# Seven block products for the first expert's second output product, with sums made by accumulating transfers

## The chip, the cores and the metric

The kernel runs on one core of one Trainium2 chip. The metric is device time in microseconds of one launch. The engines are TensorE (matmul), VectorE, ScalarE, GpSimd and SyncE; the last issues the loads. In the profile they are PE (and PEld for its weight loads), DVE, ACT, POOL and SP.

## The reference

Attention with a causal mask (2 batches, 12 heads, 448 positions, 64 per head) gives x, 896 tokens by 768. Two experts follow, one on the other's output:

```python
h = x @ w_in                    # 768 -> 2048
g = h - np.tanh(h)
x = g @ w_out                   # 2048 -> 768, the first expert
a, b = x @ w_a, x @ w_b         # 768 -> 1536 each
out = (a * b) @ w_out2          # 1536 -> 768, the second expert
```

q, k and v are float32. The experts' weights are 64-bit floats; the kernel loads their upper bytes and puts float32 values together from their bits.

## The kernel before

Every float32 operand is split into a high half (float32r) and a low half, and a product of two operands is three matmuls: high by high, high by low, low by high. ScalarE makes the high half (L292 for weights, L649 for activations), VectorE the low half (L301, L650).

The first expert's 2048 hidden columns are taken in three groups of 4, 6 and 6 chunks of 128 (`GROUPS1`, L69). For each group the hidden product is made, then its part of the output product, which is added up in `part` in SBUF. The loop over the groups is at L799. This text is about the output product of the second group, 6 chunks.

The hidden products of the second and third group use seven block products in place of eight: two row blocks (384 of the 768 inputs), two column blocks (two chunks) and two token blocks (the batches B0 and B1, 448 tokens each). A unit is a pair of chunks; `turn` (L775) makes one of its seven products, 9 matmuls of 448 columns. Which product adds to which PSUM bank is in it. `combine` (L239) makes the sums of weight blocks on VectorE, `x_sums` those of x. `gate` (L747) makes tanh on ScalarE, the difference on VectorE and then both halves of g.

The output product of the second group is plain: for each of 6 output blocks `dm` and for two pieces of tokens (512 and 384), 6 chunks by 3 matmuls, and then an addition of the PSUM bank to `part` on VectorE (`add`, L745). Its weights are whole blocks, split at a stroke (128x768).

Weights go through a chain. `load_part` (L185) loads a tile in two halves on SyncE's queue. `magnitude` (L194) makes an fp16 part on ScalarE and `bits` (L214) joins it with the lower bits on VectorE, into one of 4 buffers `t`. `split_high` and `split_low` then write the halves into one of 5 pairs of buffers `wh`, `wl`, each pair with place for two split blocks of 384 or one whole of 768. `plan` is the order in which blocks are split. `advance`, called once per product, makes one step of each. A `t` buffer is reused when `last_use` of its tile has been split.

PSUM has 8 banks with four names: `s` 4, `t` 2, `o` 1, `h` 1. `next_bank` gives them out in a fixed turn. Eight buffers `e` hold results copied from PSUM.

The attention part has an order written by hand (`ORDER`). All behind it is placed by a planner, which takes instructions in the order of the program as priorities and its own costs; each engine then executes its queue in order. In this kernel TensorE's instructions of the output product are mixed with the last products of the hidden stage. GpSimd issues no transfers and does nothing behind the attention.

Of the kernel before, what the change touches and what calls it, by code (L numbers as in the profile page):

```python
# [9 lines left out]
F32 = mybir.dt.float32  # L10
F32R = mybir.dt.float32r
# [40 lines left out]
def attention_moe_moe2(ctx, tc, q, k, v, w_in, w_out, w_a, w_b, w_o, out):  # L52
    nc = tc.nc
# [35 lines left out]
    s3p = ctx.enter_context(tc.tile_pool(name="s3", bufs=2))  # L89
# [6 lines left out]
    ident = const.tile([128, 128], F32, name="ident")  # L96
    tops = [const.tile([128, KD, 128, 2], F16, name=f"top{i}") for i in range(2)]


# [3 lines left out]
    def block(w, r, c):  # L103
        return w[r, c * W:(c + 1) * W].rearrange("(k p) n -> p k n", p=128)[:, :, 1:]
# [11 lines left out]
    def in_turn(u0, pairs_):  # L116
# [11 lines left out]
        stages.append([(u0 + u, m) for u, m in out])  # L128
        plan.extend(stages[-1])

    f0 = 0
    for g in GROUPS1:
# [12 lines left out]
    LAST = (1, 2, 5, 3, 6, 7, 4)  # L145
    homes, quads = {}, {}
    for n in range(KD // 2):
        quads[u0 + NF2 + n] = {}

# [16 lines left out]
    plan.extend((u, m) for m in LAST for u in quads)  # L166
    last_use = {}
    for j, (i, m) in enumerate(plan):
        for x in () if i in quads and m else (i,) if m is None else (units[i], units[i] + 1):
# [3 lines left out]
    thirds, summed, last_turned = {}, set(), []  # L173

    def load_part():

# [11 lines left out]
    def magnitude():  # L188
        i = at["abs"]
        if 2 * i + 1 >= at["load"] or i >= at["bits"] + len(tops):  # L190
            return
        raw, nk = raws[i]
        top = raw[:, 0:nk].bitcast(BF16).rearrange("p k (f w) -> p k f w", w=4)
        nc.scalar.copy(out=tops[i % len(tops)][:, 0:nk, :, 1], in_=top[:, :, :, 2])  # L194
        at["abs"] += 1

    def bits():

        i = at["bits"]
        while at["t"] in homes and homes[at["t"]] != "t" or last_use.get(at["t"], at["halve"]) < at["halve"]:  # L200
            at["t"] += 1
        home = homes.get(i, "t")
        held_ = sum(homes.get(x, "t") == "t" for x in range(at["t"], i))
        if i >= at["abs"] or home == "t" and held_ >= TP or home in ("th", "tl") and not last_turned:
            return
        raw, nk = raws.pop(i)
        low = raw[:, 0:nk].bitcast(I32).rearrange("p k (f w) -> p k f w", w=2)
        top = tops[i % len(tops)][:, 0:nk].rearrange("p k f w -> p k (f w)").bitcast(I32)
        if home == "t":
            ts[i] = tp.tile([128, KD, 128], I32, tag="t", name="t")[:, 0:nk]  # L210
        else:
            t = (partp if home == "part" else xtra).tile([128, NT], I32, tag=home, name="tlast")
            ts[i] = t[:, 0:KD * 128].rearrange("p (k n) -> p k n", n=128)
        nc.vector.scalar_tensor_tensor(  # L214
            out=ts[i], in0=low[:, :, :, 0], scalar=13, in1=top, op0=ALU.logical_shift_right, op1=ALU.bitwise_or
        )
        at["bits"] += 1
        if home == "part" and i in [x[2, 2] for x in quads.values()]:
            a21, a22 = [ts[i_].bitcast(F32) for x in quads.values() if x.get((2, 2)) == i for i_ in (x[2, 1], i)]
            nc.vector.tensor_tensor(out=a21, in0=a21, in1=a22, op=ALU.add)  # L220

    def quad(u, r, f):
        return ts[quads[u][r, f]].bitcast(F32)
# [3 lines left out]
    def source(j):  # L227

        i, m = plan[j]
        if m is None:  # L230
            return ts[i].bitcast(F32)
        if i in quads:
            return quad(i, *WHERE[m])
        if m == 7:
            return thirds[i]
        t = ts[units[i] + int(m in (4, 5))].bitcast(F32)
        return t[:, 3:6] if m in (2, 3, 4) else t[:, 0:3]

    def combine(u, m):  # L239

        t0, t1 = [ts[units[u] + x].bitcast(F32) for x in range(2)]
# [21 lines left out]
    def split_high():  # L263
        j = at["high"]
        if j >= len(plan):
            return
        i, m = plan[j]
        full = m is None or i in quads
        if m is not None and j > at["halve"]:
            return  # L270
        if i in quads and m is not None:
            need = quads[i][1, 1 if m == 1 else 2]
        else:
            need = i if full else units[i] + int(m not in (1, 2))
        if need >= at["bits"]:
            return
        if full:
            at["slots"] += at["slots"] % 2
        if at["slots"] % 2 == 0:
            if at["slots"] // 2 >= at["done"] // 2 + WB:  # L280
                return
            at["pair"] = [w_p.tile([128, KD, 128], F32R, tag=x, name=x) for x in ("wh", "wl")]
        if m is not None and i in quads:
            combine_quad(i, m)
        elif m in (3, 5, 6, 7):
            combine(i, m)
        x = source(j)
        nk = x.shape[1]
        k0 = 0 if full else 3 * (at["slots"] % 2)
        halves[j] = [t[:, k0:k0 + nk] for t in at["pair"]]  # L290
        at["slots"] += 2 if full else 1
        nc.scalar.copy(out=halves[j][0], in_=x)  # L292
        at["high"] += 1

    def split_low():
        j = at["halve"]
        if j >= at["high"]:
# [4 lines left out]
        at["halve"] += 1  # L302

    def split():
        split_high()
# [36 lines left out]
    def attention():  # L342
        with ExitStack() as st:
# [8 lines left out]
            pt1 = fixed.tile([QC, 2, NQ, 2, QC], F32, name="pt1")  # L352
            warm = fixed.tile([128, 512], BF16, name="warm")
            mask = fixed.tile([128, S], F32, name="mask")
            nc.vector.memset(warm, 0.0)
            nc.vector.memset(mask, 0.0)
            for top in tops:
# [225 lines left out]
    BATCHES = [slice(b * S, (b + 1) * S) for b in range(B)]  # L583
    B0, B1 = BATCHES

    def new_g(f):

        if not g_full:
            gh[f, 0], gl[f, 0] = [g_a.tile([128, S], F32R, tag=x, name=x) for x in ("gh", "gl")]
            return  # L590
        g = [g_full[0].tile([128, NT], F32R, tag=x, name=x) for x in ("gwh", "gwl")]
        gw[f] = g
        for b in range(B):
            gh[f, b], gl[f, b] = [t[:, BATCHES[b]] for t in g]

    def hidden(w, cs, hi, lo, h, act, dve):
# [4 lines left out]
        th = ep.tile([128, 512], F32, tag="e", name="e")[:, :n]  # L601
        gg = ep.tile([128, 512], F32, tag="e", name="e")[:, :n]
# [37 lines left out]
    in_attention.clear()  # L640

    g_full.append(ctx.enter_context(tc.tile_pool(name="g2", bufs=max(GROUPS1))))
    partp = ctx.enter_context(tc.tile_pool(name="part", bufs=PARTS))


# [7 lines left out]
        nc.vector.tensor_tensor(out=o, in0=a, in1=b_, op=ALU.subtract)  # L653

    def etile():
        return ep.tile([128, 512], F32, tag="e", name="e")[:, :S]
# [87 lines left out]
    def add(x, o):  # L744
        nc.vector.tensor_tensor(out=x, in0=o, in1=x, op=ALU.add)  # L745

    def gate(u, q, x, on_chip):  # L747

        f, b = 2 * u + q // 2, q % 2
# [49 lines left out]
    for gi, g in enumerate(GROUPS1):  # L799
# [14 lines left out]
        else:  # L814
            u0 = stages[gi - 1][0][0]
            for u, m in stages[gi - 1]:
                turn(u, m, lambda u, q, x, on_chip: gate(u - u0, q, x, on_chip))
# [62 lines left out]
        product(o, parts, go_on=go_on)  # L880
        at["done"] += 2

    def kept(o):
        r = etile()
        nc.scalar.copy(out=r, in_=o)
        return r

    def put(dm, cs, r):
        nc.sync.dma_start(out=out[dm * 128:(dm + 1) * 128, cs], in_=r)

# [61 lines left out]
```

## Time and profile before

| | us |
|---|---|
| median of 3 runs | 551.82 (551.16 to 552.98) |
| the profiled execution | 552.16 |
| its span | 550.4 |
| TensorE busy | 542.4 |
| VectorE busy | 439.6 |
| ScalarE busy | 335.5 |
| GpSimd busy | 65.8 |

The profile is one execution. Matmuls are pipelined: the duration in a row (0.37 us for 448 columns) is longer than the distance to the next start (about 0.2 us), so lengths of stages are read from starts. VectorE's and ScalarE's operations overlap a little in the same way.

### The profile page before, as it was taken

The numbers are of one execution on the slowest core, as the hardware profiler recorded it, in microseconds if no ns is written. First come the engines' busy times: TensorE is split into PE (matmuls) and PEld (weight loads), VectorE is DVE, ScalarE is ACT, GpSimd is POOL, SyncE is SP. The second block draws the span as 40 slices with busy tenths as digits, with TensorE's granted clock in tenths as the row PEclk, the third lists the DMA queues.
The fourth block names the chain that finished last, engine by engine and source line by source line (L and its number), as shares of the span: only waits on it lengthen the run. The fifth ranks groups of instructions, "written<-read, shape, count | busy, mean of one in ns | idle before, by whom it ended". The sixth has DMA issues, their size and how long they took to land.

```text
span 550.4 us, 8639 instructions
## 1 busy us (share of the span) xinstructions
PE 542.4 (99%) x3094; PEld 481.5 (87%) x3094; DVE 439.6 (80%) x855; ACT 335.5 (61%) x688; POOL 65.8 (12%) x88
## 2 busy tenths in 40 slices
PE   8999999999999999999999999999999999999997
PEld 4777788897899988999898999999999999999996
DVE  5897886479998976557978999879797879999840
ACT  6988996457677853246855475647564657356421
POOL 5688762200000000000000000000000000000000
PEclk9999999999999999999999999999999999999999
DMA  9725350057133733312643033537374631001011
GB/s 273 242 85 150 92 149 1 1 192 228 43 130 114 225 120 114 105 35 91 211 141 108 0 115 115 170 116 259 118 258 134 206 114 58 2 0 51 17 68 67
DMA packets 70827, 64.94 MB, mean 118 GB/s; under 512 B 13952, under 2 KB 70784, under 8 KB 70784
## 3 DMA queue, kind: packets, MB, share of 16 engines
q1 hardware_dynamic: 70784, 64.40, 36.9%
q8 instruction: 24, 0.39, 0.3%
q14 instruction: 19, 0.16, 0.1%
HBM read 61.63 MB, written 2.75 MB: 117 GB/s over the span
## 4 chain that ended last, share of the span: by engine, by line
PE 89%; DVE 4%; ACT 3%; DMA 2%; issue 1%; SPq 0%; POOL 0%; DVEq 0%; ACTq 0%
PE s L328 41%; PE t L328 17%; PE h L328 13%; PE o L328 7%; PE o L480 4%; PE s L419 3%; PE t L454 3%; ACT p L440 2%; DVE t L214 1%; DMA raw<-in_moe_w_out 1%; DVE xsum L685 1%; PE t L499 1%; ACT pt L462 1%; DMA v<-in_v 1%; DMA raw<-in_moe_w_in 1%
## 5 line engine op out<-in xcount | busy, mean ns | idle before, releaser
L292 ACT CAST wh<-t 128x384 fp32r<-128x384 f32 (+2 forms) x141 | 77.1, 577 | 48.2 <-PE s L328 22.2
L194 ACT CAST top<-raw 128x768 f16<-128x768 bf16 (+1 forms) x70 | 73.9, 1056 | 49.2 <-DMA raw<-in_moe_w_b 11.9
L301 DVE TENSOR_TENSOR wl<-t,wh 128x384 fp32r<-128x384 f32 (+2 forms) x136 | 81.7, 623 | 14.6 <-ACT wh L292 14.1
L214 DVE SCALAR_TENSOR_TENSOR t<-raw,top 128x768 int32<-128x768 int32 (+1 forms) x62 | 60.4, 988 | 2.0 <-ACT top L194 1.8
L440 ACT ACTIVATE p<-p,m 112x448 f32<-112x448 f32 (+3 forms) x96 | 49.9, 526 | 5.6 <-DVE m L431 5.3
L328 PE MATMUL s<-last,wh 128*128 128x448 f32 x168 | 48.4, 365 | 0.0
L328 PE MATMUL s<-xl,wh 128*128 128x448 f32 x120 | 44.0, 367 | 0.0
L431 DVE CUSTOM_DVE_ANT_0 p<-s,mask 112x448 f32<-112x448 f32 (+3 forms) x96 | 37.9, 440 | 7.3 <-PE s L419 6.6
L328 PE MATMUL s<-xh,wl 128*128 128x448 f32 x120 | 43.5, 366 | 0.0
L328 PE MATMUL s<-xh,wh 128*128 128x448 f32 x120 | 43.5, 366 | 0.0
L328 PE MATMUL s<-gwl,wh 128*128 128x384 f32 (+2 forms) x96 | 34.9, 366 | 0.3 <-DVE gwl L606 0.3
L328 PE MATMUL s<-gwh,wl 128*128 128x384 f32 (+2 forms) x96 | 34.9, 365 | 0.0
L328 PE MATMUL s<-gwh,wh 128*128 128x512 f32 (+2 forms) x96 | 34.4, 365 | 0.0
L328 PEld LDWEIGHTS s<-last,wh 128*128 128x128 f32 x168 | 31.5, 188 | 2.6
L328 PE MATMUL s<-last,wl 128*128 128x448 f32 x84 | 30.7, 365 | 0.0
L745 DVE TENSOR_TENSOR e<-s,e 128x448 f32<-128x448 f32 x31 | 19.2, 618 | 12.9 <-PE s L328 12.6
L454 PE MATMUL t<-ident,p 112*112 112x112 f32 x195 | 27.6, 265 | 0.2 <-ACT p L440 0.2
L462 ACT COPY pt<-t 112x448 f32<-112x448 f32 (+1 forms) x39 | 18.5, 485 | 14.2 <-PE t L454 12.3
L480 PE MATMUL o<-pt,v 112*64 112x224 f32 (+1 forms) x288 | 26.7, 326 | 0.4 <-DMA v<-in_v 0.4
L480 PEld LDWEIGHTS o<-pt,v 112*64 112x64 f32 x288 | 19.1, 136 | 7.8 <-issue 0.9
L649 ACT CAST last<-g 128x896 fp32r<-128x896 f32 x21 | 19.0, 942 | 10.4 <-PE t L328 4.5
L401 POOL TENSOR_TENSOR qkl<-qk,qkh 128x448 fp32r<-128x448 f32 x22 | 25.2, 1148 | 1.0
(219 smaller groups left out, 1464.0 us busy)
## 6 DMA issues: line engine op xcount, KB each, us to landing
raw<-in_moe_w_out SPq DMA_DIRECT2D x48, 383.2 KB, 4.1
raw<-in_moe_w_in SPq DMA_DIRECT2D x32, 383.2 KB, 4.1
raw<-in_moe_w_a SPq DMA_DIRECT2D x24, 383.2 KB, 4.1
raw<-in_moe_w_b SPq DMA_DIRECT2D x24, 383.2 KB, 4.5
raw<-in_moe_w_out SPq DMA_DIRECT2D x12, 255.5 KB, 4.5
qk<-in_q SPq DMA_DIRECT2D x12, 224.0 KB, 3.6
qk<-in_k SPq DMA_DIRECT2D x12, 224.0 KB, 3.9
v<-in_v SPq DMA_DIRECT2D x24, 112.0 KB, 3.2
```

What stands on the lines that cost most here:

```text
L194: nc.scalar.copy(out=tops[i % len(tops)][:, 0:nk, :, 1], in_=top[:, :, :, 2])
L214: nc.vector.scalar_tensor_tensor(out=ts[i], in0=low[:, :, :, 0], scalar=13, in1=top, op0=ALU.logical_shift_right, op1=ALU.bitwise_or)
L292: nc.scalar.copy(out=halves[j][0], in_=x)
L301: engine.tensor_tensor(out=lo, in0=source(j), in1=hi.bitcast(F32), op=ALU.subtract)
L328: nc.tensor.matmul(o, a, b_, start=j == 0 and not go_on, stop=j == n - 1, skip_group_check=True)
L401: nc.gpsimd.tensor_tensor(out=lo[:, x], in0=qk[i][:, x], in1=hi[:, x].bitcast(F32), op=ALU.subtract)
L431: nc.vector.tensor_tensor_reduce(out=p[:, e], in0=s, in1=mask[:QC, S - n:], scale=-scale, scalar=3.0e38, op0=ALU.add, op1=ALU.min, accum_o ...
L440: nc.scalar.activation(out=p[:, e], in_=p[:, e], func=ACTF.Exp, bias=least[i][:, c, e:e + 1], scale=-1.0, accum_out=sums[i][:, c, e:e + 1],)
L454: nc.tensor.transpose(out=pst[:QC, x * QC:(x + 1) * QC], in_=blk, identity=ident[:QC, :QC])
L462: nc.scalar.copy(out=out_, in_=in_)
L480: nc.tensor.matmul(o[64 * e:64 * e + 64, cs], vt[:, k_, e, :], p.rearrange("s c q -> s (c q)"), start=k_ == 0, stop=k_ == 2 * h + 1, skip_ ...
L745: nc.vector.tensor_tensor(out=x, in0=o, in1=x, op=ALU.add)
```

## The change

The second group's output product is made with seven block products too, and the product number is the outermost loop: product 1 for three pairs of output blocks, then product 5 for all three, and so on in the order 1, 5, 2, 3, 6, 7, 4 (`FIRST`). A block product is 3 chunks by 3 matmuls of 448 columns; there are 21.

The weights' top row is made negative when its fp16 part is made (`negative`), so that most sums become additions. These are made by transfers that GpSimd issues and that add to their destination in SBUF: S1, S2, S4 on weights, T1 to T4 on g, and the additions to `part`. Six weight tiles stay in SBUF for all of it, four in `t` and two in a new `t2`. `gate32` keeps g in float32 without halves, and `out_term` makes the halves of one term when they are wanted. For all paired weights `combine` makes the sums one at a time, when their product comes, and `thirds` goes away.

```diff
+    LAST = (1, 2, 5, 3, 6, 7, 4)
+    FIRST = (1, 5, 2, 3, 6, 7, 4)
+    homes, quads, outs, negative = {}, {}, {}, set()
...
+        if gi == 1:
+            for r in range(2):
+                for n in range(KD // 2):
+                    if r == 0:
+                        outs[len(units)] = [len(tiles)]
+                        negative.add(len(tiles))
+                        units.append(None)
+                    else:
+                        list(outs.values())[n].append(len(tiles))
+                    if 3 * r + n >= TP:
+                        homes[len(tiles)] = "t2"
+                    tiles.append(block(w_out, slice((f0 - g) * 128, f0 * 128), 2 * n + r))
+            plan.extend((u, m) for m in FIRST for u in outs)
+            continue
...
+        for u, (_, t1) in outs.items():
+            if t1 == i:
+                more(out_quad(u, 2, 1), out_quad(u, 2, 2), "S1")
+                out_sums(u)
...
+    def more(o, x, what):
+        if what in BY_DMA:
+            nc.gpsimd.dma_start(out=o, in_=x, accum_op=ALU.add)
+        else:
+            nc.vector.tensor_tensor(out=o, in0=x, in1=o, op=ALU.add)
+
+    def out_sums(u):
+        if outs[u][1] < at["bits"] and plan.index((u, 2)) < at["halve"]:
+            more(out_quad(u, 1, 1), out_quad(u, 2, 1), "S2")
+            more(out_quad(u, 1, 2), out_quad(u, 1, 1), "S4")
...
-        if m == 3:
-            nc.vector.tensor_tensor(out=a12, in0=a12, in1=a11, op=ALU.subtract)
-        elif u not in summed:
-            summed.add(u)
-            thirds[u] = s3p.tile([128, 3, 128], F32, tag="s3", name="s3")
-            nc.vector.tensor_tensor(out=thirds[u], in0=a11, in1=a21, op=ALU.subtract)
-            nc.vector.tensor_tensor(out=a21, in0=a21, in1=a22, op=ALU.add)
-            nc.vector.tensor_tensor(out=a11, in0=a21, in1=a11, op=ALU.subtract)
+        for n, ms, o, x, y, op in (
+            (1, (5, 6, 3, 7), a21, a21, a22, ALU.add), (2, (6, 3, 7), a11, a21, a11, ALU.subtract),
+            (4, (3, 7), a12, a12, a11, ALU.subtract), (3, (7,), a11, a22, a11, ALU.subtract),
+        ):
+            if m in ms and (u, n) not in summed:
+                summed.add((u, n))
+                nc.vector.tensor_tensor(out=o, in0=x, in1=y, op=op)
...
+    def gate32(u, q, x, on_chip):
+
+        f, b = 2 * u + q // 2, q % 2
+        if f not in G:
+            G[f] = g_tile("gwh", F32)
+        th = etile()
+        nc.scalar.activation(out=th, in_=x, func=ACTF.Tanh)
+        minus(G[f][:, BATCHES[b]], *((th, x) if b == f // NK else (x, th)))
...
+    def out_term():
...
+        t = g_tile("gwl")
+        hi, lo = [t[:, cs] for cs in BATCHES]
...
+        if m == 1:
+            more(b11, b12, "T1")
+        elif m == 5:
+            more(b12, b22, "T3")
+            more(b11, b22, "T2")
+        elif m == 3:
+            more(b21, b11, "T4")
...
+        for m in FIRST:
+            for n, u in enumerate(outs):
+                if m in (1, 2, 5):
+                    acc[n, m] = bank({1: "sss", 2: "tto", 5: "sht"}[m][n])[:, :S]
+                o = acc[n, {6: 1, 7: 1, 4: 1, 3: 5}.get(m, m)]
+                wh, wl = next_weights()
+                product(o, [((wh[:, k], wl[:, k]), out_terms[m, k]) for k in range(NK)], go_on=m in (3, 6, 7, 4))
...
+            if out_at[0] < len(LAST1):
+                for _ in range(NK):
+                    out_term()
...
+                if not final and u - u0 == NK - 1:
+                    for _ in range({5: 3, 7: 1, 3: 1, 4: 1}.get(m, 0)):
+                        out_term()
+            if not final:
+                outputs()
+                continue
```

Two other edits go with it: `ident` moves into a pool that is freed behind the attention, and the `e` tiles are 448 wide instead of 512. In `outputs` each finished bank is copied to an `e` tile by ScalarE (`kept`), with one subtraction (product 2) or addition (product 6) on VectorE, and a transfer adds the tile to `part`.

## Rows read from the trace of the kernel before

**Rows 1.** The page's totals: engine, busy us, share of the span, instructions.
```profile
PE 542.4 (99%) x3094; PEld 481.5 (87%) x3094; DVE 439.6 (80%) x855; ACT 335.5 (61%) x688; POOL 65.8 (12%) x88
```

**Rows 2.** Waits of TensorE, longest total first: us, times, longest us.
```profile
PE h L562 <- DVE warm L355: 1.2, 1, 1.2
...
PE t L328 <- ACT ypart L834: 0.7, 1, 0.7
...
PE s L328 <- DVE gwl L606: 0.3, 1, 0.3
```

**Rows 3.** Windows: busy us (instructions) of PE, PEld, DVE, ACT, POOL; clock, DMA share, GB/s.
```profile
155.50:234.60 79.10, 79.10 (x389) 71.24 (x388) 59.47 (x100) 43.72 (x73) 0.00 (x0) 1.00 0.43 140
...
450.00:500.00 50.00, 50.00 (x248) 46.25 (x248) 48.55 (x60) 29.23 (x41) 0.00 (x0) 1.00 0.15 49
```

**Rows 4.** Timeline of TensorE, first matmuls of runs: start, us, line, tiles, shape.
```profile
170.58 0.37 PE L328 MATMUL h<-gh,wh 128*128 128x448 f32 x1
...
172.44 0.37 PE L328 MATMUL s<-xh,wh 128*128 128x448 f32 x1
...
227.47 0.33 PE L328 MATMUL s<-gwh,wh 128*128 128x384 f32 x1
...
230.62 0.39 PE L328 MATMUL o<-gwh,wh 128*128 128x512 f32 x1
...
234.74 0.36 PE L328 MATMUL s<-xh,wh 128*128 128x448 f32 x1
...
236.56 0.36 PE L328 MATMUL t<-xh,wh 128*128 128x448 f32 x1
```

**Rows 5.** Groups by shape, 155.5 to 234.6 us (the `ypart` row: whole span).
```profile
L301 DVE TENSOR_TENSOR wl<-t,wh 128x384 fp32r<-128x384 f32 x18 | 9.4, 550 | 0.7 <-ACT wh L292 0.7
L292 ACT CAST wh<-t 128x384 fp32r<-128x384 f32 x17 | 8.2, 513 | 8.0 <-PE t L328 6.9 <-PE h L328 1.2
L650 DVE TENSOR_TENSOR gwl<-e,gwh 128x448 fp32r<-128x448 f32 x12 | 7.4, 621 | 0.5 <-ACT gwh L649 0.5
L649 ACT CAST gwh<-e 128x448 fp32r<-128x448 f32 x12 | 6.8, 565 | 2.3 <-DVE e L653 2.3
L301 DVE TENSOR_TENSOR wl<-t,wh 128x768 fp32r<-128x768 f32 x6 | 5.7, 954 | 0.3 <-ACT wh L292 0.3
L292 ACT CAST wh<-t 128x768 fp32r<-128x768 f32 x6 | 5.0, 833 | 4.5 <-PE t L328 3.7 <-PE h L328 0.4 <-PE s L328 0.4
L784 ACT COPY e<-s 128x448 f32<-128x448 f32 x3 | 1.5, 525 | 0.0
L745 DVE TENSOR_TENSOR ypart<-s,ypart x12: 548/618/692, 207.7 to 317.3; 128x384 f32<-128x384 f32 x6, 128x512 f32<-128x512 f32 x6
```

**Rows 6.** The joining of weight bits, the same stretch.
```profile
L214 DVE SCALAR_TENSOR_TENSOR t<-raw,top 128x768 int32<-128x768 int32 x14 | 13.3, 952 | 0.1
```

**Rows 7.** ScalarE's longest wait, 150 to 250 us: us in total, times, longest.
```profile
ACT wh L292 <- PE t L328: 11.7, 5, 3.7
```

**Rows 8.** DMA issues: count, KB each, median us to landing; then raw tiles, 150 to 260.
```profile
raw<-in_moe_w_out SPq DMA_DIRECT2D x48, 383.2 KB, 4.1
...
out<-e SPq DMA_DIRECT2D x12, 224.0 KB, 1.9
...
DMA to landing us min/median/max: 3.1/3.8/5.6
```

**Rows 9.** An issue on SyncE (ns min/median/max), and GpSimd's costliest group.
```profile
L185 SPq DMA_DIRECT2D raw<-in_moe_w_in x12: 367/428/1252, 183.0 to 206.4; - x12
...
L401 POOL TENSOR_TENSOR qkl<-qk,qkh 128x448 fp32r<-128x448 f32 x22 | 25.2, 1148 | 1.0
```

**Rows 10.** A bank's hand-over in the timeline: two matmuls, then VectorE's addition.
```profile
195.81 0.37 PE L328 MATMUL t<-gh,wl 128*128 128x448 f32 x1
196.02 0.37 PE L328 MATMUL h<-xh,wh 128*128 128x448 f32 x1
...
196.22 0.62 DVE L745 TENSOR_TENSOR e<-t,e 128x448 f32<-128x448 f32 x1 [2.74 <-PE t L328]
```

More of the change, by code (lines that the diff above doesn't have):

```diff
@@ L94, in bank @@
         return ps.tile([128, 512], F32, tag=tag, name=tag, bufs=BANKS[tag])
-    ident = const.tile([128, 128], F32, name="ident")
     tops = [const.tile([128, KD, 128, 2], F16, name=f"top{i}") for i in range(2)]
@@ L129, in in_turn @@
         plan.extend(stages[-1])
+    LAST = (1, 2, 5, 3, 6, 7, 4)
+    FIRST = (1, 5, 2, 3, 6, 7, 4)
+    homes, quads, outs, negative = {}, {}, {}, set()
     f0 = 0
-    for g in GROUPS1:
+    for gi, g in enumerate(GROUPS1):
         u0 = len(units)
@@ L168, in attention_moe_moe2 @@
     for j, (i, m) in enumerate(plan):
-        for x in () if i in quads and m else (i,) if m is None else (units[i], units[i] + 1):
+        for x in () if i in quads and m else (i,) if m is None else outs[i] if i in outs else (units[i], units[i] + 1):
             last_use[x] = j
@@ L193, in magnitude @@
         top = raw[:, 0:nk].bitcast(BF16).rearrange("p k (f w) -> p k f w", w=4)
-        nc.scalar.copy(out=tops[i % len(tops)][:, 0:nk, :, 1], in_=top[:, :, :, 2])
+        if i in negative:
+            nc.scalar.mul(out=tops[i % len(tops)][:, 0:nk, :, 1], in_=top[:, :, :, 2], mul=-1.0)
+        else:
+            nc.scalar.copy(out=tops[i % len(tops)][:, 0:nk, :, 1], in_=top[:, :, :, 2])
         at["abs"] += 1
@@ L210, in bits @@
             ts[i] = tp.tile([128, KD, 128], I32, tag="t", name="t")[:, 0:nk]
+        elif home == "t2":
+            ts[i] = t2p.tile([128, KD, 128], I32, tag="t2", name="t2")
         else:
@@ L233, in source @@
             return quad(i, *WHERE[m])
[L234 to L235 removed]
+        if i in outs:
+            return out_quad(i, *WHERE[m])
         t = ts[units[i] + int(m in (4, 5))].bitcast(F32)
@@ L272, in split_high @@
             need = quads[i][1, 1 if m == 1 else 2]
+        elif i in outs and m is not None:
+            need = outs[i][int(m not in (1, 2))]
         else:
@@ L302, in split_low @@
         at["halve"] += 1
+        if plan[j][0] in outs and plan[j][1] == 2:
+            out_sums(plan[j][0])
     def split():
@@ L354, in attention @@
             mask = fixed.tile([128, S], F32, name="mask")
+            ident = fixed.tile([128, 128], F32, name="ident")
             nc.vector.memset(warm, 0.0)
@@ L584, in attention_moe_moe2, with g_tile @@
     B0, B1 = BATCHES
+    def g_tile(tag, dt=F32R):
+        return g_full[0].tile([128, NT], dt, tag=tag, name=tag)
     def new_g(f):
@@ L600, in hidden @@
         yield from matmuls(h, [((wh[:, kk], wl[:, kk]), (xh[kk][:, cs], xl[kk][:, cs])) for kk in range(KD)])
-        th = ep.tile([128, 512], F32, tag="e", name="e")[:, :n]
-        gg = ep.tile([128, 512], F32, tag="e", name="e")[:, :n]
+        th = ep.tile([128, S], F32, tag="e", name="e")[:, :n]
+        gg = ep.tile([128, S], F32, tag="e", name="e")[:, :n]
         act(lambda: nc.scalar.activation(out=th, in_=h, func=ACTF.Tanh))
@@ L655, in etile @@
     def etile():
-        return ep.tile([128, 512], F32, tag="e", name="e")[:, :S]
+        return ep.tile([128, S], F32, tag="e", name="e")[:, :S]
     def small(n=1):
@@ L745, in add @@
         nc.vector.tensor_tensor(out=x, in0=o, in1=x, op=ALU.add)
+    G = {}
+    def gate32(u, q, x, on_chip):
[5 more added lines that the diff above has]
+        minus(G[f][:, BATCHES[b]], *((th, x) if b == f // NK else (x, th)))
+    LAST1 = [m for m in FIRST for _ in range(NK)]
+    out_terms, out_at = {}, [0]
+    def out_term():
+        n = out_at[0]
+        out_at[0] += 1
+        m, kk = LAST1[n], n % NK
+        b11, b12, b21, b22 = [f in G and G[f][:, cs] for f in (kk, kk + NK) for cs in BATCHES]
+        x = {1: b11, 2: b21, 5: b11, 3: b22, 6: b11, 7: b12, 4: b21}[m]
+        t = g_tile("gwl")
+        hi, lo = [t[:, cs] for cs in BATCHES]
+        if m == 6:
+            nc.scalar.mul(out=hi, in_=x, mul=-1.0)
+            nc.vector.scalar_tensor_tensor(
+                out=lo, in0=x, scalar=-1.0, in1=hi.bitcast(F32), op0=ALU.mult, op1=ALU.subtract
+            )
+        else:
+            halve(hi, lo, x)
+        out_terms[m, kk] = hi, lo
+        if m == 1:
[5 more added lines that the diff above has]
+            more(b21, b11, "T4")
@@ new lines, in kept, with outputs @@
+    def kept(o):
+        r = etile()
+        nc.scalar.copy(out=r, in_=o)
+        return r
+    def outputs():
+        acc = {}
+        for m in FIRST:
[5 more added lines that the diff above has]
+                product(o, [((wh[:, k], wl[:, k]), out_terms[m, k]) for k in range(NK)], go_on=m in (3, 6, 7, 4))
+                top, low = [part[2 * n + r] for r in range(2)]
+                if m == 1:
+                    if "q0" in BY_DMA:
+                        c1[n] = kept(o)
+                    else:
+                        add(top[:, B0], o)
+                elif m == 2:
+                    if "q0" in BY_DMA:
+                        minus(c1[n], c1[n], o)
+                        more(top[:, B0], c1[n], "q0")
+                    else:
+                        minus(top[:, B0], top[:, B0], o)
+                elif m == 6:
+                    if "q1" in BY_DMA:
+                        c2[n] = kept(o)
+                        add(c2[n], acc[n, 5])
+                        more(top[:, B1], c2[n], "q1")
+                    else:
+                        add(top[:, B1], o)
+                        add(top[:, B1], acc[n, 5])
+                elif m in (5, 7, 4):
+                    what = {5: "q3a", 7: "q3b", 4: "q2"}[m]
+                    e = kept(o) if what in BY_DMA else o
+                    more(low[:, BATCHES[int(m != 4)]], e, what)
+                at["done"] += 1
+                advance()
+            if out_at[0] < len(LAST1):
+                for _ in range(NK):
+                    out_term()
@@ L881, in all_of @@
         at["done"] += 2
[L883 to L886, printed above, removed]
     def put(dm, cs, r):
```

17 lines of the change are left out of this document (12 added, 5 removed).

## The prediction

> **What bounds the kernel now.** I read the page's totals first [rows 1]: TensorE is busy for 542.4 of 550.4 us at full clock, VectorE for 80%, ScalarE for 61%, and GpSimd only early. Busy TensorE alone proves little, so next come its waits [rows 2]. The largest adds up to 1.2 us and belongs to the start; in the experts' stages only two show, of 0.7 and 0.3 us. Then the stages [rows 3]: from 155.5 to 234.6 us (the first expert's second hidden and second output product) TensorE never pauses, VectorE is busy for 59.5 of 79.1 us and ScalarE for 43.7. Last the timeline [rows 4]: consecutive matmuls start at an even pitch, 9 of 448 columns in 1.86 us (170.58 to 172.44) or 1.82 (234.74 to 236.56). So TensorE's stream sets the end, and what is taken from it in this stage comes off the end as long as no wait takes its place. All later stages are as dense (450 to 500 us: 50.00 of 50 [rows 3]), so an earlier end of this stage shifts everything behind it.
>
> **What is removed from TensorE.** The output product has 6 blocks of 18 matmuls with 512 columns and 18 with 384. A run of 18 takes 4.12 us (230.62 to 234.74) and 3.15 us (227.47 to 230.62) [rows 4], so 6 x 7.27 = 43.6 us. The new one has 7 products x 3 column pairs = 21, each of 9 matmuls with 448 columns: 21 x 1.82 to 1.86 = 38.2 to 39.1, I take 38.6. Gain 5.0 us, between 4.6 and 5.4.
>
> **VectorE and ScalarE** [rows 5]. VectorE loses 6 low halves of a whole block (954 ns), 12 low halves of g (621) and 12 additions to `part` (618): 5.7 + 7.5 + 7.4 = 20.6 us. It gains 21 low halves of weights (550), 3 subtractions for product 7 (550), 21 low halves of terms (621), 6 subtractions or additions at products 2 and 6 (about 620): 11.6 + 1.7 + 13.0 + 3.7 = 30.0. Net 9.4 more, so 68.9 us in a stretch of 79.1 - 5.0 = 74.1: 93%. ScalarE loses 6 x 833 and 12 x 565 ns, 11.8 us, and gains 21 x 513 (high halves), 21 x 565 (terms) and 15 x 525 (`kept`), 30.5: net 18.7, 62.4 of 74.1, 84%. The cover is that both run beside TensorE; another stage shows VectorE at 48.55 of 50 us with TensorE full [rows 3]. So I cost this at nothing; it is late only through order, which is the first rival. The new order of `combine` has the same four operations per unit, and `ident`, the narrower `e` tiles and the missing `s3` tiles issue nothing: nothing for all of these.
>
> **The weight tiles are held longer.** Six tiles of the second output product stay until product 4 is split, and the four `t` buffers with them. The next hidden tile gets a buffer only when the low half of (first pair, product 4) is made; then follow 0.95 (bits), 0.51 (high) and 0.55 (low), 2.0 us [rows 5, 6], its fp16 part being made before. Splits run ahead of TensorE by up to five buffer pairs, 10 products, 18.6 us at 1.86. That the lead is full shows in ScalarE's waits: `wh` waited for TensorE 11.7 us in five waits [rows 7]; it was held up by buffers that TensorE still read. 2.0 fits into 18.6: nothing.
>
> **36 accumulating transfers from GpSimd.** Nine on weights (S1, S2, S4 for three pairs), 12 on g (T1 to T4 for three chunks), 15 on `part`. The trace has none. Bounds by the nearest rows [rows 8]: a store of 224 KB lands in 1.9 us, a load of 383 KB in 4.1 (up to 5.6 in this stretch). An accumulation reads a source and the destination and writes, so I put the top at a load and a store together, 6.0, and take 4.1, for the load row also has a source that is not in plain order. Issuing one costs GpSimd between 0.43 us (SyncE's load issue) and 1.15 (its own 128x448 operation) [rows 9]: 36 of them make 15 to 41 us in 74 on an engine otherwise idle here, so the engine is no bound.
>
> What waits for them? T1 runs from the low half of a product 1 term to the high half of the product 5 term; three products of the last hidden unit and three of product 1 lie between, 6 x 1.86 = 11.2 us, above 4.1 and 6.0. T2, T3 and T4 have at least as many. S1 must land before product 5's weights; within the 18.6 us lead it is hidden. The chain is S2 and then S4 for each of three pairs. They go through one in-order queue, and S4 waits for S2, so behind a waiting S4 stand the next pair's S2 and the transfers of T and `part`. At worst the third pair's product 3 weights come 6 x 4.1 = 24.6 us after product 2's first split. TensorE wants them 5 products later plus its lead: 9.3 + 18.6 = 27.9. Hidden, with 3.3 us to spare; the limit is 27.9 / 6 = 4.65 us for one landing.
>
> The Trainium skill (DMA: Bandwidth & Descriptors, "Anatomy of one DMA — SWDGE (gpsimd) path") gives about 2 us plus bytes over 436 GB/s for such a transfer; for 229,376 bytes that is an estimate of 2.5 us, the chain would be 15 us and the sum the same. Against the change speaks the same skill's Collectives: The Full Stack ("The bandwidth ceiling: the fold count and why AG ≠ RS ≠ AR"): an addition in a DMA engine reads two sources and so runs at half the rate of a copy; the estimate grows to 3.1 us, still under the limit. No row here shows an accumulation; the 1.9 and 4.1 us lie on both sides of these.
>
> **PSUM and the new waits.** Product 1 holds three `s` banks to the end of the stage; product 5 holds the fourth `s`, the `h` and one `t`; product 2 needs `t`, `t`, `o`. So its second pair must wait until VectorE has drained the first from the only free `t`. The price is in the trace [rows 10]: a product's last matmul starts at 195.81 and hands over at 196.02; VectorE's addition from that bank starts at 196.22 and takes 0.62, so the bank is free 0.8 us after. It costs nothing if the third pair (bank `o`) is put first. I count 0.8. Terms have six buffers, so a product's three terms can begin when TensorE leaves the product two before: 3 x 0.565 and a low half of 0.62 make 2.3 us, against 5.6 us (3 products). 3.3 us of slack: nothing.
>
> **Sum**, against the profiled execution's own 552.16 us (span 550.4): 552.16 - 5.0 + 0.8 = 548.0. The median of the runs shown is 0.34 lower, so 547.6. Its own range: 546.4 (gain 5.4, no bank wait) to 549.5 (two more waits of the first rival's size).
>
> **Rivals.** *ScalarE and VectorE queue in order, and the terms come late.* For: they rise to 84 and 93%, and a split that waits for a sum in ScalarE's queue holds back the terms and `kept` copies behind it. One landing of 4.1 against 3.3 of slack is 0.8 us; at each of the five products after the first two, 4.0 to 4.3 us: 551.8. VectorE says the same: it was idle for 19.6 of 79.1 us; if half of that (9.8) can't be filled, 68.9 + 9.8 = 78.7 leaves 0.4 of the gain. Against: the stage at 48.55 of 50 kept TensorE full. *The sums on GpSimd's queue become the path* (the other side). The place is S2 and S4 ahead of product 3; it decides from 4.65 us per landing. At 6.0: 36.0 - 27.9 = 8.1 us of idle TensorE, 547.6 + 8.1 = 555.7; at 5.6, 5.7 us and 553.3. For: no accumulation is in the trace, 15 other transfers share the queue, loads move 140 GB/s meanwhile [rows 3]. Against: the store's 1.9 us, and S2 needs product 1's split alone, so it may run earlier. *No stall at all*: 546.8 in the profile's terms; it lies in the forecast's range. *The gain is made and given back later*: a denser later stage would need a bound other than TensorE; its lack of waits [rows 2] speaks against it, and I give it no chance of its own.
>
> **Chances.** Forecast 0.55, late terms 0.20, sums on the path 0.25. What a measurement of this kernel can tell from no change is about 0.3%, 1.7 us, so faster means below 550.2, slower above 553.5. Late terms lie at 549.5 to 553, of which 0.07 falls faster, 0.11 same, 0.02 slower; of the sums on the path 0.04 same, 0.21 slower. Faster 0.62, same 0.15, slower 0.23. The range goes from 546.2 to 555.5: about 0.05 is left out below and 0.13 above, where the landing is over 6 us.
>
> **What would show it.** Right: TensorE's matmuls 27 fewer; no wait of it over 1 us between 180 and 235 us, and one of about 0.8 at product 2 on bank `t`; accumulating transfers that land in under 4.65 us; ScalarE and VectorE near 84 and 93% there. Wrong: TensorE waiting for `wl` or `wh` at product 3 (sums), or for `gwl` tiles at each new product (late terms); ScalarE's casts with idle time ended by a DMA; a landing over 4.65 us; a gap at the change from the hidden to the output product, which I gave none.

## The result, and the profile after

The changed kernel takes 555.15 us (median of 7 runs, 553.75 to 558.62) against 552.44 for the kernel before, measured beside it (7 runs); the ratio of all runs is 1.0067, 95% interval [1.0051, 1.0083] (the two medians alone give 1.0049). It is slower by 2.7 us where 5 us faster was forecast. The profiled execution took 554.76 us, its span is 553.0.

The totals of the page, against [rows 1]:
```profile
PE 540.3 (98%) x3067; PEld 478.0 (86%) x3067; DVE 446.3 (81%) x876; ACT 351.1 (63%) x727; POOL 97.1 (18%) x124
```
TensorE has the 27 matmuls fewer (3067 against 3094), but its busy share fell, so it waits. TensorE's waits, against [rows 2]:
```profile
PE t L375 <- ACT wh L337: 1.9, 2, 1.8
PE s L375 <- DVE gwl L824: 1.4, 1, 1.4
...
PE s L375 <- ACT gwl L701: 1.1, 1, 1.1
...
PE s L375 <- ACT e L840: 0.4, 1, 0.4
```
These waits are new, all in the changed stage. Their places, in TensorE's timeline: the first three pairs are the last matmul before a gap and the first behind it.
```profile
196.56 0.36 PE L375 MATMUL t<-gh,wl 128*128 128x448 f32 x1
197.99 0.47 PE L375 MATMUL s<-gwl,wh 128*128 128x448 f32 x1 [1.07 <-ACT gwl L701]
...
214.85 0.87 PE L375 MATMUL s<-gwl,wh 128*128 128x448 f32 x3
217.14 0.47 PE L375 MATMUL s<-gwl,wh 128*128 128x448 f32 x1 [1.42 <-DVE gwl L824]
...
221.91 0.36 PE L375 MATMUL s<-gwl,wl 128*128 128x448 f32 x1
224.04 0.47 PE L375 MATMUL t<-xh,wh 128*128 128x448 f32 x1 [1.77 <-ACT wh L337]
...
224.56 0.76 PE L375 MATMUL s<-gwl,wh 128*128 128x448 f32 x2
...
225.11 0.57 PE L375 MATMUL s<-gwl,wl 128*128 128x448 f32 x1
225.49 0.95 PE L375 MATMUL s<-gwl,wh 128*128 128x448 f32 x2
```
Beyond the even pitch, 1.2 us are lost inside product 5 (its third term waits for T1), 1.6 inside product 6 (the low half of a term), and 1.9 at 222 us. There two matmuls of the *next* stage (`t<-xh`, `t<-xl`) stand in TensorE's queue ahead of product 7, which starts at 224.56, and their weights aren't there. Product 7 could not have begun earlier either: it adds to a bank that ScalarE copied until 224.42 us. The last pair shows starts 0.38 us apart where 0.21 is usual. All gaps and slow starts from 183 to 235 us add up to 8.7 us: 552.16 - 5.0 + 8.7 = 555.9, against 554.76 measured. The gain was made, and more than lost again within the stage.

The low half that product 6 waits for, in the timelines of ScalarE and VectorE:
```profile
214.22 1.04 ACT L823 ACTIVATE gwl<-gwh 128x448 fp32r<-128x448 f32 x2
...
214.20 1.48 DVE L346 TENSOR_TENSOR wl<-t,wh 128x384 fp32r<-128x384 f32 x3
215.61 0.94 DVE L232 SCALAR_TENSOR_TENSOR t<-raw,top 128x768 int32<-128x768 int32 x1
216.48 1.14 DVE L824 SCALAR_TENSOR_TENSOR gwl<-gwh,gwl 128x448 fp32r<-128x448 f32 x2
```
The first high half was there at 214.80 us. VectorE began its low half at 216.48, behind three low halves of weights and one joining of bits.

Windows, first the kernel before, then the kernel after; columns as in [rows 3]:
```profile
180.00:240.00 60.00, 60.00 (x297) 53.96 (x296) 42.55 (x70) 29.18 (x47) 0.00 (x0) 1.00 0.41 132
```
```profile
180.00:240.00 60.00, 55.13 (x253) 47.16 (x253) 45.23 (x82) 39.20 (x78) 27.85 (x32) 0.97 1.00 214
210.00:220.00 10.00, 8.53 (x41) 7.27 (x40) 10.00 (x20) 6.56 (x14) 5.25 (x7) 1.00 1.03 196
220.00:230.00 10.00, 7.87 (x31) 6.25 (x30) 8.18 (x17) 6.07 (x11) 1.75 (x2) 0.83 1.10 295
```
The column to look at is the last but one: the 16 DMA engines went from 0.41 to 1.00. VectorE and ScalarE are far from full over the 60 us, but VectorE is busy for all of the ten us in which product 6 waits for it. The granted clock is 0.83 in the ten us around the gap at 222; behind the gaps of 1.6 and 1.9 us TensorE ran at the lower of its two levels (starts 0.37 us apart, 448 columns at 1.2 GHz), and the seven slow starts make 1.1 of the 8.7 us.

The DMA part of the page, after; the issue of a transfer on GpSimd (ns); and the landing of raw weight tiles issued from 205 to 232 us, against the last row of [rows 8]:
```profile
q1 hardware_dynamic: 70784, 64.40, 36.7%
q0 software_dynamic: 5184, 7.96, 8.8%
...
raw<-in_moe_w_in SPq DMA_DIRECT2D x32, 383.2 KB, 5.4
...
ypart<-e POOLq DMA_DIRECT2D x15, 224.0 KB, 5.7
...
gwh<-gwh POOLq DMA_DIRECT2D x12, 224.0 KB, 3.8
...
t<-t POOLq DMA_DIRECT2D x9, 192.0 KB, 4.6
...
L248 POOL DMA_DIRECT2D t<-t x9: 859/862/880, 180.8 to 205.3; - x9
...
DMA to landing us min/median/max: 5.5/8.8/10.6
```
A sum on g lands in 3.8 us in the median, one on weights in 4.6, near the 4.1 that I took, and an addition to `part` in 5.7. But from 205 to 232 us the loads of weights need 8.8 us in the median, where the kernel before had 3.9 (3.8 over the longer stretch of [rows 8]). Those of the next stage's hidden product are also issued later. SyncE's issues of these 12 half tiles, before and then after (start, us over which they are spread):
```profile
182.97 23.87 SPq L185 DMA_DIRECT2D raw<-in_moe_w_in  x12
```
```profile
180.52 40.51 SPq L198 DMA_DIRECT2D raw<-in_moe_w_in  x12
```
The last went out at 206.8 before and at 221.0 after, since six weight tiles stay in their buffers: a load waits until the joining of bits has freed a raw tile, at the longest 24.5 us where it was 13.7, and the joining needs a `t` buffer. ScalarE's timeline around the gap at 222 us, after:
```profile
221.10 1.08 ACT L210 CAST top<-raw 128x768 f16<-128x768 bf16 x1 [2.22 <-DVE wl L346]
222.04 1.12 ACT L701 CAST gwl<-gwh 128x448 fp32r<-128x448 f32 x2
223.07 0.92 ACT L337 CAST wh<-t 128x384 fp32r<-128x384 f32 x2
223.90 0.52 ACT L840 COPY e<-s 128x448 f32<-128x448 f32 x1
226.79 1.06 ACT L210 CAST top<-raw 128x768 f16<-128x768 bf16 x1 [2.38 <-DMA raw<-in_moe_w_in]
227.72 0.51 ACT L840 COPY e<-s 128x448 f32<-128x448 f32 x1
```
ScalarE's queue stands for 2.2 us ahead of a `top` cast, which needs a raw tile. The view names VectorE, but the last thing that the cast needs of VectorE (a joining of bits from the same `top` buffer) had ended by 219.0 us, while the second half of its raw tile landed at 221.0. Behind it come the `wh` casts that TensorE waits for and the `kept` copy of product 7's bank. At 226.8 the same happens again, and the `kept` copy behind it makes TensorE's wait of 0.4 us at 228, 0.7 beyond the pitch. With the 1.9 us at 222 and the 1.1 of the lower clock, late raw tiles make 3.7 of the 8.7 us.

### The profile page after: what moved, and what is told of

Its sections match the earlier page's. It is cut to its first block, busy times and chain, and to the rows that moved or that the text cites. A ratio compares the mean times of both kernels' runs of the same rounds, so it can differ in the third digit from the quotient of the medians.

```text
span 553.0 us, 8743 instructions
## 1 busy us (share of the span) xinstructions
PE 540.3 (98%) x3067; PEld 478.0 (86%) x3067; DVE 446.3 (81%) x876; ACT 351.1 (63%) x727; POOL 97.1 (18%) x124
## 3 DMA queue, kind: packets, MB, share of 16 engines
q1 hardware_dynamic: 70784, 64.40, 36.7%
q0 software_dynamic: 5184, 7.96, 8.8%
## 4 chain that ended last, share of the span: by engine, by line
PE 84%; DMA 7%; ACT 4%; issue 2%; DVE 2%; SPq 0%; POOL 0%; ACTq 0%; DVEq 0%; POOLq 0%
PE s L375 39%; PE t L375 14%; PE h L375 10%; PE o L375 8%; PE o L528 4%; PE s L467 4%; PE t L502 3%; DMA raw<-in_moe_w_in 3%; DMA t<-t 2%; ACT p L488 1%; DMA raw<-in_moe_w_out 1%; ACT wh L337 1%; PE t L547 1%; PE h L502 1%; DVE wl L346 1%
## 5 line engine op out<-in xcount | busy, mean ns | idle before, releaser
L337 ACT CAST wh<-t 128x384 fp32r<-128x384 f32 (+2 forms) x174 | 90.3, 555 | 37.8 <-PE s L375 27.2
L346 DVE TENSOR_TENSOR wl<-t,wh 128x384 fp32r<-128x384 f32 (+2 forms) x169 | 96.0, 594 | 17.2 <-ACT wh L337 17.1
L210 ACT CAST top<-raw 128x768 f16<-128x768 bf16 (+1 forms) x67 | 70.4, 1053 | 47.2 <-DMA raw<-in_moe_w_b 14.0
L375 PE MATMUL s<-gwl,wh 128*128 128x448 f32 (+2 forms) x144 | 48.0, 378 | 2.9 <-DVE gwl L824 1.4
L293 DVE TENSOR_TENSOR t<-t 128x384 f32<-128x384 f32 x72 | 39.0, 549 | 0.2
L375 PEld LDWEIGHTS s<-gwl,wh 128*128 128x128 f32 x144 | 27.3, 192 | 7.6 <-DVE gwl L824 1.8
L502 PEld LDWEIGHTS t<-ident,p 112*112 112x112 f32 x195 | 19.8, 133 | 6.1 <-ACT pt L510 1.6
```

Source lines behind the costliest of these rows:

```text
L293: nc.vector.tensor_tensor(out=o, in0=x, in1=y, op=op)
L375: nc.tensor.matmul(o, a, b_, start=j == 0 and not go_on, stop=j == n - 1, skip_group_check=True)
L502: nc.tensor.transpose(out=pst[:QC, x * QC:(x + 1) * QC], in_=blk, identity=ident[:QC, :QC])
```

## The experiments

Each was timed in five rounds beside the kernel before. "Lost" is TensorE's time beyond the even pitch around the stage (about 170 to 252 us) in the profiled execution; "loads" is the median landing of raw tiles issued from 205 to 232 us.

| | us | ratio to before, interval | lost | loads |
|---|---|---|---|---|
| the change | 555.15 | 1.0067 [1.0051, 1.0083] | 8.7 | 8.8 |
| e1, GpSimd adds itself | 565.38 | 1.0246 [1.0226, 1.0266] | 16.1 | 4.9 |
| e2, S on VectorE | 555.32 | 1.0056 [1.0034, 1.0078] | 7.8 | 7.8 |
| e3, T on VectorE | 549.56 | 0.9960 [0.9945, 0.9975] | 1.9 | 4.4 |
| e4, additions to `part` on VectorE | 556.12 | 1.0078 [1.0055, 1.0101] | 8.4 | 3.9 |
| e5, T1 on VectorE | 553.94 | 1.0046 [1.0025, 1.0066] | 7.7 | 5.2 |
| e6, T2 to T4 on VectorE | 552.52 | 1.0001 [0.9981, 1.0020] | 3.5 | 4.2 |
| e7, T and S on VectorE | 550.88 | 0.9975 [0.9960, 0.9990] | 3.4 | 4.5 |
| e8, all transfers short | 550.33 | 0.9965 [0.9949, 0.9981] | 2.1 | 4.0 |
| e9, before with idle transfers | 551.62 | 0.9989 [0.9976, 1.0002] | 0 | 4.4 |
| e10, before with new `combine` | 551.92 | 0.9994 [0.9981, 1.0007] | 0 | 3.5 |
| e11, T and q0 on VectorE | 552.46 | 1.0014 [1.0001, 1.0027] | 5.7 | 4.0 |
| e12, T, q3b and q2 on VectorE | 548.47 | 0.9939 [0.9916, 0.9962] | 1.9 | 4.4 |
| e13, `part` transfers short | 557.87 | 1.0102 [1.0083, 1.0120] | 9.6 | 6.0 |
| e14, S and T transfers short | 554.58 | 1.0034 [1.0015, 1.0052] | 7.7 | 6.8 |
| e15, T, q1, q3b and q2 on VectorE | 553.75 | 1.0030 [1.0013, 1.0046] | 6.9 | 4.0 |

The kernel before had a median of 551.79 to 552.50 in these sessions. Every edit lets the planner place the stage anew, so an experiment changes more than its line.

**e1.** `more` calls GpSimd's own addition:
```diff
-            nc.gpsimd.dma_start(out=o, in_=x, accum_op=ALU.add)
+            nc.gpsimd.tensor_tensor(out=o, in0=x, in1=o, op=ALU.add)
```


> All 36 sums as additions that GpSimd computes itself, in place of transfers. Theory A (the transfers fill the DMA engines, whose share was 0.92 to 1.10 from 180 to 240 us, so loads and sums land late and ScalarE's queue stalls): share falls to about 0.45, loads land in about 4.1 us again, GpSimd is busy for 36 x 1.0 to 1.15 = 36 to 41 us more than its early part, TensorE's lost time in 183 to 235 us falls from 8.6 to under 3 us, time 547 to 550. Theory B (the stalls come from the added work and its order on ScalarE and VectorE, whoever makes the sums): 553 to 557, with waits for gwl and wh of the same size.

The share fell, as A says, but both theories missed a new limit. The window, and two groups by shape from 183.5 to 240 us (their mean is the number behind the busy time):
```profile
180.00:240.00 60.00, 51.04 (x231) 44.08 (x230) 60.00 (x74) 35.21 (x70) 45.17 (x28) 0.94 0.33 105
...
L346 DVE TENSOR_TENSOR wl<-t,wh 128x384 fp32r<-128x384 f32 x25 | 21.7, 904 | 0.0
L248 POOL TENSOR_TENSOR ypart<-e,ypart 128x448 f32<-128x448 f32 x9 | 19.8, 2221 | 6.8 <-DVE e L705 6.8
```
VectorE is busy for all 60 us: its low halves take 904 ns where they took 550 [rows 5], beside GpSimd's additions, and nine of these take 2221 where an operation of that size took 1148 [rows 9]. The run tells nothing on transfers.

**e2 to e4, one group of sums back to VectorE.** Names are taken out of `BY_DMA`: S1, S2, S4; or T1 to T4; or all the q's.

> Only the nine sums on weights (S1, S2, S4) go back to VectorE (9 x 0.55 = 5 us more there). Theory A with the chain S2, S4 as the main part: no cast wh waits for a transfer (3.5 us before), time 551 to 553. If the bytes of the other 27 transfers are what counts: 554 to 556, loads still over 5 us. Theory B: VectorE gets fuller, 555 to 558.

> Only the twelve sums on g (T1 to T4) go back to VectorE (12 x 0.62 = 7.4 us more there). Theory A: the wait of TensorE for product 5's term (1.1 us at 197 us, behind T1) goes, share about 0.8, time 552 to 554. Theory B: 556 to 559, since VectorE had about 5 us free in the stage.

> Only the fifteen additions to part go back to VectorE, from PSUM (15 more operations, 9.3 us; 15 copies of 0.53 us fewer on ScalarE). These are 3.4 of the 8.0 MB of the transfers. Theory A with the bytes as the main part: loads land in under 5 us, no clock drop behind 220 us, time 550 to 553. Theory B: VectorE has 78 us of work in 79: 556 to 560.

e2 gave nothing, as expected if the other transfers' bytes count: loads still need 7.8 us, and the gap at 222 is 4.4 us long. Taking the chain S2, S4 off the queue does not bring the time back. e3 gave back 5.6 us, more than either theory said, with VectorE at 54.3 of 60 us: VectorE's load as a whole is not the limit. TensorE's waits in e3 from 170 to 250 us (the first matmul of the next stage is idle for 0.2 us, 0.3 beyond the pitch), and the landing of raw tiles:
```profile
PE t L375 <- DVE gwl L702: 0.3, 1, 0.3
PE t L375 <- ACT wh L337: 0.2, 1, 0.2
...
DMA to landing us min/median/max: 3.3/4.4/7.6
```
e4 missed theory A and lies at the lower end of theory B, not because VectorE is full (51.3 of 60 us): loads landed early (3.9 us), yet TensorE lost 3.3 us to T1's term and 2.4 to a bank that VectorE drains late in its queue.

**e5 and e6, T1 or the rest of T.** The same edit with T1 alone, or T2, T3 and T4.

> Only T1 (three of the twelve sums on g, the ones just ahead of product 5) goes to VectorE; T2, T3, T4 stay transfers. Theory A1 (the time goes into waits on single sums: a transfer with its place in GpSimd's queue and its landing lies ahead of product 5's terms): nearly all of the gain of moving all twelve, 549.5 to 551.5. Theory A2 (the time goes into the bytes: the DMA engines are full and everything lands late): a quarter of it, 553 to 555.

> T2, T3 and T4 (nine sums on g) go to VectorE, T1 stays a transfer. Theory A1: a wait of TensorE for product 5's term of 1 to 3 us stays, 552.5 to 555. Theory A2: three quarters of the gain, 550 to 552.

Moving T1 gave 1.2 us, the other nine 2.6, of the 5.6 for all twelve. e5 lies where A2 put it. e6 lies at the lower end of A1's range and outside A2's, but without the wait that A1 names (0.3 us for a term). And e5 lost 4.2 us anew at two places whose weights waited for transfers of S. So the two decide nothing between the theories.

**e7 and e8, no waited sum by transfer; all transfers short.**
```diff
-            nc.gpsimd.dma_start(out=o, in_=x, accum_op=ALU.add)
+            n = 1 if what[0] == 'S' else 128; nc.gpsimd.dma_start(out=o[:, 0:n], in_=x[:, 0:n], accum_op=ALU.add)
```


> T and S sums (21) go to VectorE, only the additions to part are transfers, on which no product waits. Theory A1: no sum is waited for through a transfer, as fast as with T alone or faster, 548 to 550. Rival B (VectorE's load): 5 us more on VectorE than with T alone, 550.5 to 553.

> All 36 transfers stay and keep their order of issue and their waits as far as the planner lets them, but each moves only 512 of 1536 or 1792 bytes per partition; the rest of each sum is left out. Theory A2 (bytes): DMA share from about 1.0 to 0.65 in 180 to 240 us, sums and loads land in 3 to 4 us, time 548 to 551. Theory A1 (queue and fixed landing time): the sums still land in 3 us or more, 552.5 to 555.

e7 lies where rival B put it, 1.3 us behind e3. e8 keeps all 36 issues and still gives back 4.8 of the 7.5 us between the change (555.15) and the forecast (547.6), as A2 said. It doesn't tell apart the load on the DMA engines, the earlier landing of the sums (2.4 us on g and `part`) and the planner's order; the pair e8 and e14 below does so for one gap.

**e9 and e10, parts of the change in the kernel before.** e9 issues, behind each addition to `part`:
```diff
+                        for _ in range(3):
+                            idle.append(idle.pop(0))
+                            nc.gpsimd.dma_start(
+                                out=idle[-1], in_=part[dm][:, cs.start:cs.start + 384], accum_op=ALU.add
+                            )
```


> The kernel before with 36 accumulating transfers of 192 KB more in its output product, three behind each addition to part, into tiles that nothing reads (and with combine, e tiles and s3 as changed, for room). No product waits on them. Theory A2 (full DMA engines delay the loads and all that waits for them): share from 0.41 to about 0.8 in 180 to 240 us, raw tiles land in 5 us or more instead of 3.9, and the time is 552.5 to 555 as far as loads are wanted at once. Theory A1 (only waits on the sums themselves cost): 551.5 to 552.8, loads late but hidden.

> The kernel before with the new order of combine alone (sums one at a time, thirds gone). My prediction counted this edit at nothing: 551.5 to 553. If it has a part in the slower time: 553.5 or more.

e10 is the same as before: the new order of `combine` costs nothing, as I said. e9 is as A1 put it. Its window, and the landing of its transfers:
```profile
180.00:240.00 60.00, 60.00 (x298) 54.21 (x297) 42.23 (x70) 29.26 (x47) 17.45 (x20) 1.00 0.78 191
...
idle<-ypart POOLq DMA_DIRECT2D x36, 192.0 KB, 5.3
```
The DMA engines are at 0.78, from 210 us on at 0.84 to 1.04 in each ten us, and TensorE loses nothing. But the raw tiles landed in 4.4 us: their loads went out in pairs 8 to 10 us apart, much as before, where the change issued six half tiles from 214.3 to 221.0. So a nearly full share alone made neither late loads nor waits; e9 has no late loads to show what these cost.

**e11, e12 and e15, toward a faster version.** q0 is the additions of products 1 and 2, q1 of 6, q3b of 7, q2 of 4. The text on record for e12 names q1 too; the kernel that ran left q1 a transfer, so it moved 1.4 MB, not 2.1.

> As the change with T on VectorE, and the additions of products 1 and 2 to part (q0) on VectorE too, from PSUM. 0.7 MB of transfers fewer, three operations more on VectorE, three copies fewer on ScalarE. Theory A2: 548 to 550, as T alone (549.6) or better. Rival B (VectorE's queue): 550.5 to 553.

> As the change with T on VectorE, and the additions of products 6, 7 and 4 to part (q1, q3b, q2) on VectorE too. 2.1 MB of transfers fewer at the stage's end, when the next stage's loads run; nine to twelve operations more on VectorE. Theory A2: 547.5 to 549.5. Rival B: 550.5 to 554.

> The change with T and the additions of products 6, 7 and 4 to part (q1, q3b, q2) on VectorE; S, q0 and q3a stay transfers. Against the fastest so far (T, q3b and q2 on VectorE, q1 a transfer; 548.5): 0.7 MB of transfers fewer and three operations more on VectorE at product 6. If transfers still cost there: 547.5 to 548.5. If VectorE's queue is now the limit: 549 to 552.

e12 is the fastest, 0.61% under the kernel before. e11 lies in rival B's range for another reason: it lost 1.4 us at 200 and 2.1 at 210 us to weights, whose casts waited 8.2 us in all for transfers of S. e15 is slower than both of its ranges. The next stage's first matmuls had their weights, but product 7 waited for a bank that VectorE drained late:
```profile
220.39 0.37 PE L375 MATMUL t<-xl,wh 128*128 128x448 f32 x1
223.73 1.11 PE L375 MATMUL s<-gwl,wh 128*128 128x448 f32 x2 [2.98 <-DVE ypart L797]
```

**e13 and e14, short transfers by kind.** The edit of e8, for q alone or for S and T alone.

> The change with only the 15 additions to part cut to 512 of 1792 bytes per partition (the rest of these sums is left out); S and T whole. If the bytes on the DMA engines are what counts (2.5 of 8.0 MB gone, none of them waited for): 551 to 553.5. If the landing of the sums that are waited for counts: 554 to 556.

> The change with only the S and T sums cut to 512 bytes per partition (the rest of these sums is left out); the additions to part whole. If the landing of the sums that are waited for counts: they land in about 2.5 to 3 us, 550 to 552, as with all cut (550.3). If bytes count whoever waits: 552 to 554.

Both theories missed both. The gap of e13; behind it, its landing of raw tiles:
```profile
222.41 0.37 PE L375 MATMUL s<-gwl,wl 128*128 128x448 f32 x1
226.70 0.74 PE L375 MATMUL t<-xh,wh 128*128 128x448 f32 x1 [3.92 <-ACT wh L337]
...
DMA to landing us min/median/max: 4.0/6.0/6.8
```
It is the gap of the changed kernel, in the same place, twice as long. Up to it, every engine but ScalarE executes the same instructions in the same order in both. The planner put a second `top` cast ahead of the `wh` casts in ScalarE's queue, and that one waited for its raw tile until 224.3 us. Here the planner's order cost more than the earlier landing gave.

e8 and e14 are a cleaner pair. Up to the end of this gap all five engines execute the same instructions in the same order in both; only the bytes of the 15 additions to `part` differ, 64 KB in e8 and 224 KB in e14. The first matmul of the next stage, ScalarE's waits of `top` casts for raw tiles from 180 to 240 us, and the landing of raw tiles, first e8, then e14:
```profile
222.39 0.47 PE L375 MATMUL t<-xh,wh 128*128 128x448 f32 x1 [0.66 <-ACT wh L337]
...
ACT top L210 <- DMA raw<-in_moe_w_in: 3.0, 3, 1.2
...
DMA to landing us min/median/max: 3.1/4.0/6.3
```
```profile
223.79 0.47 PE L375 MATMUL t<-xh,wh 128*128 128x448 f32 x1 [3.56 <-ACT wh L337]
...
ACT top L210 <- DMA raw<-in_moe_w_in: 5.8, 4, 2.6
...
DMA to landing us min/median/max: 4.9/6.8/9.0
```
The six half tiles of the next stage, issued within 3.5 us in e8 and 4.3 in e14, land in 3.3 to 6.3 us in e8 and in 5.0 to 9.0 in e14. Two `top` casts ahead of the `wh` casts wait 0 and 0.9 us in e8, 2.6 and 1.2 in e14, and the gap is 0.8 or 3.7 us beyond the pitch; behind it the clock falls to its lower level in e14 alone. The times are 550.33 and 554.58. So with the order fixed, the bytes of the transfers delay the loads, and through ScalarE's queue they make this gap.

The gap is there in all four kernels whose loads landed in 6.0 us or more (the change 1.9 us, e2 4.4, e13 4.1, e14 3.7). In the nine other variants of the changed kernel that use transfers, with loads at 3.9 to 5.2 us, the same matmul waited 0.2 to 1.4 us. Between these the planner's order differs too (one to three `top` casts stand ahead of that matmul from 208 us on), so the sizes are no measure of the loads alone.

## Why the prediction was wrong

The stretch [rows 3] was read rightly: TensorE is the bound, and its stream got shorter by what I said; e3 and e12 with little loss left come to 549.6 and 548.5. Point by point:

1. *Removed from TensorE, 5.0 us.* Right: 27 matmuls fewer, and 552.16 - 5.0 + lost time meets each profile within 2 us.
2. *VectorE and ScalarE at nothing.* Right as a bound: 45.2 and 39.2 of 60 us after, less than the 93 and 84% that I had, and e3 works with VectorE at 54.3. The order on VectorE cost 1.6 us at product 6 (point 5). `combine` at nothing is shown by e10.
3. *"The weight tiles are held longer. ... nothing."* This step failed first. I followed the first tile of the next stage, whose raw data were there already, through 2.0 us of casts, and compared that with a full lead. But the buffers hold back the tiles after it: SyncE's 12 issues took 40.5 us in place of 23.9, so the loads are issued when their data are nearly due, and what waits for one of them is ScalarE's in-order queue, with the first tile's `wh` casts and the copy of product 7's bank behind it: 3.7 of the 8.7 us lost.
4. *"36 accumulating transfers"*: the landing was sized well for sums on g and weights (3.8 and 4.6 us against 4.1), less so for additions to `part` (5.7, single ones up to 8.6, over my limit of 4.65); GpSimd's issue was right (0.86 us, between 0.43 and 1.15). What is missing from the sum is the DMA engines. I priced each transfer for those who wait for it, and none for the loads that share 16 engines: the share went from 0.41 to 1.00 and late loads from 3.9 to 8.8 us. The row was at hand: 7.96 MB more, at the loads' rate, in a stage at 0.43 [rows 3]. e8 against e14 shows it at one gap: with the order the same, 2.5 MB of transfers fewer make it 0.8 us in place of 3.7. e9 points to step 3 as the other half: there a share near 1.0 left loads that go out in spaced pairs at 4.4 us.
5. *T1 has 11.2 us, terms have 3.3 us of slack.* Wrong at products 5 and 6, 1.2 and 1.6 us. T1 of the last chunk went out only at 191.4 us, in GpSimd's queue behind two transfers of S, of which the first had waited until 186.6 for another to land, and it landed 6.0 us later; why GpSimd stood for the last 2.1 us before this issue the profile doesn't tell. Product 6's low half stood in VectorE's queue behind weights. The rival of late terms had the mechanism, at two products and not five.
6. *0.8 us for product 2's bank.* Not seen: the planner mixed the third pair's matmuls in, and no start there is over 0.2 us late.
7. *The rival "the sums become the path" had 555.7 us.* The number is near, the mechanism isn't it: TensorE lost at most 0.5 us at product 3, and e2, which takes S off the queue, is as slow. Its mechanism shows in two variants: weights that waited for S cost 4.2 us in e5 and 3.5 in e11.
8. Nothing in the prediction had the clock. Idle stretches cost twice here: 1.1 us more by starts at the lower level.
9. The forecast's own range doesn't quite follow from its terms: two more waits of 0.8 us on 547.6 give 549.2, not 549.5. Nothing hangs on it.

So two steps failed together: tiles held longer were priced at nothing, and so was the load of the transfers on the DMA engines. Of the 8.7 us lost, 3.7 hang on the late loads, 2.8 are the waits of point 5 on GpSimd's and VectorE's queues, and the rest are slow starts and short waits. What stays open is why single variants with no more transfers differ by 3 to 4 us (e11 and e15 against e3). Their gaps are named above, but they lie at different places, since the planner lays each anew with its own costs. Only e8 and e14 separate its order from the transfers, and only up to one gap. No run gave the held tiles more room, so the part of step 3 is read from the timelines and from e9.

## What to carry to other kernels

Before a change adds transfers, add their bytes to the share of the DMA engines in that stage, and ask which loads then land late and in which in-order queue the wait for them stands. A buffer that is held longer must be followed to the issue of the loads behind it, not only to the next cast. Where a planner lays each variant anew, compare the order of each engine's queue first: a pair with the same order (e8 and e14) tells more than many without. And when the sums are moved, move those with an immediate reader to an engine that has room (here T to VectorE): e12, with all S, and of the additions to `part` q0, q1 and q3a, as transfers, is 0.61% faster than the kernel before.

## What the runs showed of the hardware

An addition in a transfer took the DMA engines about twice the time of a load of its bytes: 7.96 MB took 8.8% of 553 us, 163 GB/s, while the loads' 64.40 MB took 36.7%, 317 GB/s. From 180 to 240 us alone it is 162 against 327 (6.59 MB in 67.7%, 6.23 in 31.8%). This agrees with the half rate that the Trainium skill gives for additions (Collectives: The Full Stack, "The bandwidth ceiling: the fold count and why AG ≠ RS ≠ AR"); I had used it for the landing and not for the engines' share. With 512 bytes per partition (e8) an addition to `part` lands in 2.4 us in the median (2.3 to 5.4), a sum on g in 2.4, one on weights in 3.6. Side by side, GpSimd's and VectorE's additions both ran slower (e1): VectorE's low halves took 904 ns beside them and 549 behind 300 us in the same run, and GpSimd's additions to `part` 2221, where its own operation of that size took 1148 [rows 9]. The granted clock was 0.83 from 220 to 230 us (the lower level from 224.8 to 228.2), behind gaps of 1.6 us at 215 and 1.9 us at 222. Without a wait, matmuls of 448 columns started 0.207 us apart in the kernel before from 160 to 190 us and 0.203 from 220 to 250, at a granted clock of 1.00; in e8 and e14, in the same order, 0.207 and 0.203 from 160 to 190. Sums of stages from one execution carry that 2%.
